# The first MLP layer of the last block as seven half products, with the bank's halves shared by two engines

## The chip, the cores and the metric

The kernel runs on 1 core of one Trainium2 chip (trn2). The metric is the device time of one execution in microseconds (us). Engines are called PE (TensorE matmul), PEld (its weight loads), DVE (VectorE), ACT (ScalarE), POOL (GpSimd) and SP (the engine whose queue issues most transfers).

## The reference

Pooled attention, then a residual MLP block over tokens (batch 8, 576 tokens, 512 features):

```python
a1 = alpha1 * x + beta1                       # x: the attention's output, (8, 576, 512)
tok = np.einsum('ts,bsd->btd', w_tok, a1)
u = x + lam * tok
a2 = alpha2 * u + beta2
ch = np.maximum(a2 @ w_ch1, 0.0) @ w_ch2      # w_ch1: (512, 2048), w_ch2: (2048, 512)
return (u + lam * ch).astype(np.float32)
```

The change concerns `np.maximum(a2 @ w_ch1, 0.0)` for the last 512 tokens. Beta2's share is a column of biases, `bias_cols`, and alpha2 is multiplied into the weights.

## The kernel before

The 8 x 576 tokens are cut into 36 chunks of 128 and the chunks into `NBLK` = 9 blocks of 512 tokens. For each block n the kernel runs the first MLP layer and then the second. While block n runs its MLP, the attention of batch n + 1 is worked in between; blocks 7 and 8 (the last) have no attention beside them any more.

The order is written out by hand: the loop over n (L943 to L1019) collects pairs (due time, function) in `todo`, sorts them, and calls the functions in that order. Every engine runs its own instructions in that order, and the framework puts in semaphore waits where two instructions touch the same tile. A due time is only a place in the order.

**First layer, `mlp_A` (L652).** The inputs are `u_fm[n]` (features on partitions, four tiles cc of 128 features, 512 tokens, bf16) and the weights `w1` in three tensors. Hidden unit group j (16 groups of 128) takes four matmuls (L662) of 512 columns into one PSUM bank `ps_h` from a ring of six (`gp`), then one ScalarE ReLU (L669) of 128x512 into `H4[n, j // 4]` (bf16). PSUM has six banks in the ring `gp` and two in a ring "ch".

**Second layer (from block `FIRST` = 2 on).** It is done in seven half products: `weight_sum` (L723, done once) and `hidden_sum` (L744) build sums of quarter matrices on VectorE, `product` (L758) runs 16 matmuls (L785) of 256 columns for each of seven products, so 112 for a block, and `gather` (L789) adds a PSUM bank to the residual `u_sb` (L803 of 512 columns, L800 of 256). `hidden_sum` S3, S1, S2, S4 exist for g = 0 (hidden groups 0 to 3 and 8 to 11) and g = 1 (4 to 7 and 12 to 15); each is one VectorE instruction (L754) of 128x1024 bf16, some in place in the hidden tiles.

In the last block the order of the products is 1, 2, 6, 5, 7, 4, 3; the output is stored in parts, and the last transfer ends the execution.

In the first layer of block 8 nothing but matmuls, ReLUs and hidden sums of g = 0 runs; at its start VectorE does the last two gathers of block 7.

Of the kernel before, what the change touches and what calls it, by code (L numbers as in the profile page):

```python
# [7 lines left out]
FP = mybir.dt.float32  # L8
F16 = mybir.dt.float16
BF = mybir.dt.bfloat16  # L10
AF = mybir.ActivationFunctionType
ALU = mybir.AluOpType
AX = mybir.AxisListType

P = 128
SPG = 72
DM = 512
DFF = 2048
NJ = DFF // P
# [4 lines left out]
def kernel(  # L24
# [18 lines left out]
    nc = tc.nc  # L43
    ctx.enter_context(tc.manual_schedule())
    B, H, S, D = q.shape

    const = ctx.enter_context(tc.tile_pool(name="const", bufs=1))
    work = ctx.enter_context(tc.tile_pool(name="work", bufs=1))
    psA = ctx.enter_context(tc.tile_pool(name="psA", bufs=6, space=bass.MemoryType.PSUM))
    psB = ctx.enter_context(tc.tile_pool(name="psB", bufs=2, space=bass.MemoryType.PSUM))  # L50

    def gp(name):
        return psA.tile([P, 512], FP, tag="gp", name=name)
# [8 lines left out]
    NBLK = len(chunks) // 4  # L62
# [156 lines left out]
    start = const.tile([1, 2], FP, tag="start", name="start")  # L219
# [38 lines left out]
    for i in range(4):  # L258
        if i < 2:
            t = const.tile([SPG, 4, 66], F16, tag=f"vp1_{i}", name=f"vp1_{i}")  # L260
            nc.vector.memset(t, 8.0)
            vp1_pool.append(t)
            t = const.tile([P, 2, 4, SPG], BF, tag=f"kpT_{i}", name=f"kpT_{i}")
# [3 lines left out]
    for i in range(2):  # L267
        t = const.tile([SPG, 4, S + 64], F16, tag=f"ET_{i}", name=f"ET_{i}")
# [8 lines left out]
                            op0=ALU.mult)  # L277
    nc.vector.tensor_tensor(out=pool_vr[0:32, 64:72], in0=pool_v[0:32, 0:16:2],
                            in1=pool_v[0:32, 1:16:2], op=ALU.add)
# [65 lines left out]
    def setup_wtok_odd():  # L345
# [6 lines left out]
    w1 = [const.tile([P, 4, 512 * (w1_at[i + 1] - w1_at[i])], BF, tag=f"w1_{i}", name=f"w1_{i}")  # L352
          for i in range(3)]
    w2 = [const.tile([P, 4, DM], BF, tag=f"w2_{g}", name=f"w2_{g}") for g in range(4)]

    def w1_of(cc, j):
        g = j // 4
        t, c0 = (w1[0], 512 * g) if g < 2 else (w1[g - 1], 0)
        return t[:, :, c0:c0 + 512].rearrange("p c (m i) -> p c i m", i=4)[:, cc, j % 4, :]
# [17 lines left out]
    bias_cols = const.tile([P, NJ], FP, tag="bias_cols", name="bias_cols")  # L377
# [209 lines left out]
    u_fm = {}  # L587
# [56 lines left out]
    H4 = {}  # L644
# [6 lines left out]
    def mlp_A(n, j, t0=0, t1=512):  # L651

        if t0 == 0:
            ps_A[j] = gp("ps_h")
        ps_h = ps_A[j]
        one = t1 < 512
        for cc in range(4):
            if n == 0:
                rhs = u_fm[0][:, cc, 0, 0:257] if one else u_fm[0][:, cc, t0 // 256:2, 0:256]
            else:  # L660
                rhs = u_fm[n][:, cc, :]
            nc.tensor.matmul(out=ps_h[:, t0:t1 + one], lhsT=w1_of(cc, j), rhs=rhs,  # L662
                             start=(cc == 0), stop=(cc == 3))
        if one:
            nc.vector.tensor_copy(out=bias_cols[:, j:j + 1], in_=ps_h[:, 256:257])  # L665
            return
        if (n, j // 4) not in H4:
            H4[n, j // 4] = work.tile([P, 4, 512], BF, tag="H4", bufs=4, name="H4")
        nc.scalar.activation(out=H4[n, j // 4][:, j % 4, :], in_=ps_h, func=AF.Relu,  # L669
                             bias=bias_cols[:, j:j + 1], scale=1.0)  # L670

    ps_ch = {}

    def mlp_B(n, m, part):
# [69 lines left out]
    def hidden_sum(n, i, g):  # L744

        lo, hi, S2, S3 = H4[n, g], H4[n, g + 2], wino["S2"][g], wino["S3"][g]
        top, low = slice(0, HALF), slice(HALF, DM)
        o, a, b, op = {
            3: (S3, lo[:, :, top], lo[:, :, low], ALU.subtract),
            1: (lo[:, :, low], lo[:, :, low], hi[:, :, low], ALU.add),  # L750
            2: (S2, lo[:, :, low], lo[:, :, top], ALU.subtract),
            4: (lo[:, :, top], hi[:, :, top], S2, ALU.subtract),
        }[i]
        nc.vector.tensor_tensor(out=o, in0=a, in1=b, op=op)  # L754
# [34 lines left out]
    def gather(n, i, part=0):  # L789

        U = u_of[n]
        top, low = slice(0, 2), slice(2, 4)
        L, R = slice(0, HALF), slice(HALF, DM)
        rows, cols = {1: ((top, L),), 2: ((top, L),), 4: ((low, L),), 5: ((low, R),),
                      6: ((top, R),), 3: ((top, R),), 7: ((low, R), (low, L))}[i][part]
        key = {1: "V", 6: "V", 7: "V", 2: "X", 4: "Y", 5: "Z", 3: "Z"}[i]
        if key == "Z" and n == NBLK - 1:
            for pp in range(2):
                o = U[:, rows.start + pp, cols]
                nc.vector.tensor_tensor(out=o, in0=o, in1=banks[key][pp], op=ALU.add)  # L800
            return
        o = U[:, rows, cols]
        nc.vector.tensor_tensor(out=o, in0=o, in1=banks[key, "both"], op=ALU.add)  # L803
# [138 lines left out]

    for n in range(NBLK):  # L943
        todo = []
        for j in range(0 if n else 4, NJ):
            if n == 0 and j < 8:
                todo.append((j, lambda j=j: mlp_A(0, j, 0, 256)))
                todo.append((j + (1.01 if j < 7 else 0.3), lambda j=j: mlp_A(0, j, 256, 512)))
            else:
                at = 8 * (j // 4 % 2) + 4 * (j // 8) + j % 4 if n >= FIRST else j  # L950
                todo.append((at, lambda j=j: mlp_A(n, j)))
# [19 lines left out]
        if n >= FIRST:  # L971
            last = n == NBLK - 1
            when = ((3, (4.6, 14.6)), (1, (8.6, 18.86)), (2, (8.8, 18.98)), (4, (22.3, 23.0)))
            if last:
                when = ((3, (4.6, 12.6)), (1, (8.6, 16.1)), (2, (8.8, 16.2)), (4, (18.6, 19.6)))
            for i, at in when:
                for g in range(2):
                    todo.append((at[g], lambda i=i, g=g: hidden_sum(n, i, g)))
            order = (1, 2, 6, 5, 7, 4, 3) if last else (1, 2, 4, 5, 6, 3, 7)
            for s, i in enumerate(order):  # L980
                for pp in range(2):
                    todo.append((16 + 2 * s + pp, lambda i=i, pp=pp: product(n, i, pp)))
                for part in range(2 if i == 7 else 1):
                    todo.append((17.05 + 2 * s + (1.9 if i == 1 and not last else 0) + 0.01 * part,
                                 lambda i=i, part=part: gather(n, i, part)))
            if last:
                for m in range(2):
                    todo.append((19.1, lambda m=m: store(n, m, 0, HALF)))
                    todo.append((25.2, lambda m=m: store(n, 2 + m, HALF, DM)))
                    todo.append((27.2, lambda m=m: store(  # L990
                        n, 2 + m, 0, HALF, (nc.sync, nc.scalar))))
                    todo.append((29.2, lambda m=m: store(
                        n, m, HALF, DM, ((nc.sync, nc.scalar)[m],) * 2)))
            else:
                for m in range(4):
                    todo.append((27.2 if m < 2 else 29.2, lambda m=m: store(n, m)))
# [5 lines left out]
        b = n + 1  # L1002
# [47 lines left out]
```

## Time and profile before

| | |
|---|---|
| median of 3 runs | 334.12 us (333.59 to 334.47) |
| profiled execution | 334.57 us, span of its instructions 332.9 us, mean granted clock 0.993 |
| PE busy | 325.5 us, 98% of the span, 2531 matmuls |
| DVE busy | 234.5 us, 70% |
| ACT busy | 175.6 us, 53% |
| first layer of block 7 / of block 8 | 13.81 us / 13.81 us |
| second layer of block 7 / of block 8 | 12.23 us / 12.24 us |
| from the last matmul's end to the end of the span | 3.7 us |

Times inside the profile are counted from the first instruction. The ends of matmuls are modelled: consecutive matmuls of 512 columns start 0.216 us apart though each is shown with 0.38 us, and those of 256 columns 0.11 us apart though each is shown with 0.27 us. "Slot" means the distance of the starts. PEclk is the granted share of the TensorE clock.

### The profile page before, as it was taken

The page shows a single profiled execution, that of the slowest core. Times are in us where ns is not written, and L with a number is a line of the kernel's source. Part 1 is how long each engine was busy: PE and PEld are TensorE (multiplying, and loading weights), DVE is VectorE, ACT ScalarE, POOL GpSimd, SP SyncE. Part 2 cuts the span into 40 slices and gives each one's busy share as a digit, 9 for nine tenths or more (in the row PEclk, how much of TensorE's full clock was granted, in tenths as well). Part 3 has the DMA queues.
Part 4 walks back from the last instruction along what each step waited for, and adds up shares of the span by engine and source line. Part 5 has one row for each costly group of instructions (what it writes and reads, how often), then busy time and mean ns, then how long its engine had stood idle before and what let it go on. Part 6 is the DMA issues. An engine that isn't in the chain of part 4 may idle for free.

```text
span 332.9 us, 6509 instructions
## 1 busy us (share of the span) xinstructions
PE 325.5 (98%) x2531; PEld 209.2 (63%) x2531; DVE 234.5 (70%) x485; ACT 175.6 (53%) x322; POOL 94.8 (28%) x110
## 2 busy tenths in 40 slices
PE   6999999999999999999999999999999999999995
PEld 2667754455544567656775676558765866586584
DVE  6674189999769969677967797877778783263263
ACT  3584989448522871288128812682268325703710
POOL 8667828601237001900271027102510200000000
PEclk9799999999999999999999999999999999999999
DMA  8999979994994983399549943996340045003003
GB/s 117 198 210 270 271 159 206 208 227 87 146 246 105 211 159 121 72 223 181 152 89 219 182 136 73 187 189 194 61 140 2 0 61 145 2 0 127 1 32 97
DMA packets 66472, 45.81 MB, mean 138 GB/s; under 512 B 34397, under 2 KB 57061, under 8 KB 66442
## 3 DMA queue, kind: packets, MB, share of 16 engines
q1 hardware_dynamic: 52092, 32.67, 42.8%
q0 software_dynamic: 13824, 12.40, 22.8%
q8 instruction: 20, 0.33, 0.4%
q10 hardware_dynamic: 526, 0.34, 0.4%
q14 instruction: 10, 0.08, 0.1%
HBM read 38.30 MB, written 9.44 MB: 143 GB/s over the span
## 4 chain that ended last, share of the span: by engine, by line
PE 90%; DMA 5%; DVE 2%; POOL 1%; issue 0%; SPq 0%; ACTq 0%; ACT 0%; DVEq 0%; POOLq 0%
PE ps_h L662 36%; PE ps_w L785 26%; PE ps_tok L614 11%; PE ps_ch L682 7%; DMA rem_raw<-in_k_dram 3%; PE ps_s L513 2%; PE ps_av L556 2%; DMA rem_raw<-in_q_dram 2%; PE ps_kp L445 1%; PE ps_sc L493 1%; PE ps_r L520 1%; DVE x_tm L564 1%; PE ps_av L560 1%; DVE xs L578 0%; SPq L148 0%
## 5 line engine op out<-in xcount | busy, mean ns | idle before, releaser
L662 PE MATMUL ps_h<-u_fm,w 128*128 128x512 bf16 (+2 forms) x608 | 133.7, 369 | 0.2 <-DVE bias_cols L665 0.2
L669 ACT ACTIVATE H<-ps_h,bias_cols 128x512 bf16<-128x512 f32 x144 | 98.2, 688 | 56.4 <-PE ps_h L662 55.4
L662 PEld LDWEIGHTS <-w 128*128 128x128 bf16 x608 | 65.5, 114 | 49.8 <-issue 2.4
L785 PEld LDWEIGHTS <-H 128*128 128x128 bf16 x560 | 53.5, 98 | 10.8 <-DVE u_sb L803 1.2
L622 ACT CAST u_bf<-u_sb 128x512 bf16<-128x512 f32 x32 | 19.8, 618 | 70.9 <-issue 39.9
L785 PE MATMUL ps_w<-w_l,H 128*128 128x256 bf16 x448 | 53.6, 273 | 0.0
L803 DVE TENSOR_TENSOR u_sb<-u_sb,ps_w 128x512 f32<-128x512 f32 x54 | 36.3, 682 | 17.1 <-PE ps_w L785 17.1
L578 POOL TENSOR_TENSOR xs<-x_tm,lamal_bc 128x512 bf16<-128x512 f32 x12 | 15.5, 1297 | 108.8 <-DVE x_tm L564 108.7
L614 PE MATMUL ps_tok<-xs,wtT 128*128 128x512 bf16 (+3 forms) x200 | 44.9, 380 | 0.5 <-DVE xs L578 0.5
L618 DVE TENSOR_TENSOR u_sb<-x_tm,ps_tok 128x512 f32<-128x512 f32 (+1 forms) x40 | 27.3, 682 | 10.0 <-PE ps_tok L614 9.9
L564 DVE TENSOR_TENSOR x_tm<-ps_av,rec 128x320 f32<-128x320 f32 x64 | 31.4, 491 | 2.7
L542 ACT ACTIVATE ET<-ps_s 72x512 f16<-72x512 f32 x56 | 32.3, 591 | 0.0
L614 PEld LDWEIGHTS <-wtT 128*128 128x128 bf16 (+3 forms) x200 | 17.3, 100 | 16.8 <-issue 1.1
L562 DVE RECIPROCAL rec<-ps_av 128x5 f32<-128x5 f32 x64 | 12.1, 190 | 17.0 <-PE ps_av L560 16.7
L483 DVE TENSOR_TENSOR v_u<-v_u 72x1024 f32<-72x1024 f32 (+1 forms) x24 | 22.7, 948 | 0.2
L785 PE MATMUL ps_w<-w_t,h_s 128*128 128x256 bf16 x168 | 22.6, 272 | 0.0
L682 PEld LDWEIGHTS <-H 128*128 128x128 bf16 x128 | 11.9, 98 | 13.7 <-issue 0.4
L754 DVE TENSOR_TENSOR H<-H,H 128x1024 bf16<-128x1024 bf16 x14 | 9.7, 690 | 14.3 <-ACT H L669 14.2
L785 PEld LDWEIGHTS <-h_s 128*128 128x128 bf16 x168 | 16.4, 98 | 4.1
L187 POOL TENSOR_TENSOR k_bf<-k_raw 128x512 bf16<-128x512 f32 x14 | 18.4, 1317 | 1.1
L754 DVE TENSOR_TENSOR h_s<-H 128x1024 bf16<-128x1024 bf16 x21 | 14.4, 686 | 6.0 <-ACT H L669 5.8
L185 POOL TENSOR_TENSOR k_raw<-k_raw 128x512 f32<-128x512 f32 x14 | 18.4, 1316 | 0.6 <-DMA k_raw<-in_k_dram 0.6
(148 smaller groups left out, 369.0 us busy)
## 6 DMA issues: line engine op xcount, KB each, us to landing
out_dram<-u_sb SPq DMA_DIRECT2D x29, 256.0 KB
k_raw<-in_k_dram SPq DMA_DIRECT2D x12, 512.0 KB
v_u<-in_v_dram SPq DMA_DIRECT2D x12, 512.0 KB
q_bf<-in_q_dram POOLq DMA_DIRECT2D x16, 256.0 KB, 7.0
w<-in_moe_w_ch_dram POOLq DMA_DIRECT2D x6, 512.0 KB, 12.0
out_dram<-u_sb SPq DMA_DIRECT2D x11, 128.0 KB
w<-in_moe_w_ch_dram POOLq DMA_DIRECT2D x1, 1024.0 KB, 14.3
k_raw<-in_k_dram POOLq DMA_DIRECT2D x2, 512.0 KB, 16.7
```

The source lines that it names most:

```text
L483: nc.vector.tensor_tensor(out=out, in0=t[:, :, 0:width], in1=t[:, :, width:2 * width], op=ALU.add)
L542: nc.scalar.activation(out=o, in_=i, func=AF.Exp, bias=0.0, scale=0.125)
L564: nc.vector.tensor_tensor(out=x[:, 1 - odd:6 - odd, dd:dd + D], in0=av[:, :, 0:64], in1=rec.unsqueeze(2).to_broadcast((P, 5, D)), op=ALU.mult)
L614: nc.tensor.matmul(out=ps_tok[p0:p1], lhsT=wtT[0:kk, at, P * c:P * c + p1 - p0], rhs=xs_pool[i][0:kk, sc, :], start=(sc == 0), stop=(sc == 4))
L618: nc.vector.tensor_tensor(out=s["u"][p0:p1, :], in0=x[p0:p1, 1 + c if c < 4 else 5 - 5 * i, :], in1=ps_tok[p0:p1, 0:DM], op=ALU.add)
L622: nc.scalar.copy(out=s["u_bf"], in_=s["u"])
L662: nc.tensor.matmul(out=ps_h[:, t0:t1 + one], lhsT=w1_of(cc, j), rhs=rhs, start=(cc == 0), stop=(cc == 3))
L669: nc.scalar.activation(out=H4[n, j // 4][:, j % 4, :], in_=ps_h, func=AF.Relu, bias=bias_cols[:, j:j + 1], scale=1.0)
L682: nc.tensor.matmul(out=ps, lhsT=H_of(n, j)[:, 128 * m:128 * m + 128], rhs=(w2l if n else w2)[j // 4][:, j % 4, :], start=(j == 0), stop=(j ...
L754: nc.vector.tensor_tensor(out=o, in0=a, in1=b, op=op)
L785: nc.tensor.matmul(out=ps, lhsT=stat(j), rhs=moving(j), stop=(j == 7), start=(first and (pp == 0 or alone) and j == 0), skip_group_check=True)
L803: nc.vector.tensor_tensor(out=o, in0=o, in1=banks[key, "both"], op=ALU.add)
```

## The change

The first layer of the last block is done in seven half products too. The weight matrix is cut into quarters a11, a12 (hidden units 0 to 1023, feature halves) and a21, a22 (hidden units 1024 to 2047), the tokens' matrix into b11, b12, b21, b22 (feature halves by token halves of 256). For a pair of hidden groups r and r + 8 (r = 0 to 7) there are two PSUM banks of the ring of six: C for group r and V for group r + 8, each with a low half (tokens 0 to 255) and a high half; and a bank Y of the two others.

- `first_sum` makes four sums of weights (S1 = a21 + a22, S2 = S1 - a11, S3 = a11 - a21, S4 = a12 - S2), each in two VectorE instructions of 128x1024 bf16; `token_sum` makes four sums of tokens (T1 = b12 - b11, T2 = b22 - T1, T3 = b22 - b12, T4 = b21 - T2) of 128x512 bf16. These twelve instructions are put into block 7's order.
- `first_product(i, r)` is one of seven products, two matmuls of 256 columns each: 1 = a11 b11 into V low, 6 = S2 T2 and 7 = S3 T3 added to V low, 4 = a22 T4 added to V low after add2 has read it, 5 = S1 T1 into Y, 2 = a12 b21 added to C low, 3 = S4 b22 added to C high.
- `first_add(i, r)`, after product 1: copy V low to C low (VectorE, `i` = 0, "copy" below). After 6: C high = V low + Y ("add1"). After 7: V high = V low + Y ("add2"). Y is copied to SBUF by ScalarE (`i` = 3) first.
- `first_relu` makes the hidden tile from a whole bank, on ScalarE, or for the upper groups of r = 1 and 4 on VectorE.

In the order, round r has product 1(r), copy(r), product 7(r-1), add2(r-1), product 5(r), Y's copy (r), product 3(r-1), lower ReLU (r-1), product 6(r), add1(r), product 2(r), product 4(r-1), upper ReLU (r-1). Round 0 lacks the parts of r-1, and a ninth round has only them. The hidden sums of g = 0 of the last block get later due times (S3, S1, S2 in the rounds 5, 6 and 7), those of g = 1 follow the rounds. The changed program has 48 matmuls more, 38 VectorE instructions more and 6 ScalarE instructions more; the instructions of POOL and SP stay the same, in the same order.

```diff
@@ -668,6 +668,85 @@
             H4[n, j // 4] = work.tile([P, 4, 512], BF, tag="H4", bufs=4, name="H4")
         nc.scalar.activation(out=H4[n, j // 4][:, j % 4, :], in_=ps_h, func=AF.Relu,
                              bias=bias_cols[:, j:j + 1], scale=1.0)
+
+    fin = {}
+
+    def first_sum(i, g):
+
+        if "W" not in fin:
+            fin["W"] = [work.tile([P, 4, 2, 512], BF, tag="v_u", bufs=2, name="w1_s")
+                         for _ in range(2)]
+            fin["X"] = work.tile([P, 4, 2, 256], BF, tag="k_raw", bufs=2, name="u_s")
+        S = [fin["W"][q][:, 2 * r + g] for q in range(2) for r in range(2)]
+        cols = slice(512 * g, 512 * g + 512)
+        a11, a12 = w1[0][:, 0:2, cols], w1[0][:, 2:4, cols]
+        a21, a22 = w1[1 + g][:, 0:2, :], w1[1 + g][:, 2:4, :]
+        o, a, b, op = {1: (S[0], a21, a22, ALU.add), 2: (S[1], S[0], a11, ALU.subtract),
+                       3: (S[2], a11, a21, ALU.subtract), 4: (S[3], a12, S[1], ALU.subtract)}[i]
+        nc.vector.tensor_tensor(out=o, in0=a, in1=b, op=op)
+
+    def token_sum(i):
+
+        X, T = u_fm[NBLK - 1], [fin["X"][:, q] for q in range(4)]
+        b11, b12, b21, b22 = (X[:, 2 * r:2 * r + 2, 256 * q:256 * q + 256]
+                              for r in range(2) for q in range(2))
+        o, a, b = {1: (T[0], b12, b11), 2: (T[1], b22, T[0]), 3: (T[2], b22, b12),
+                   4: (T[3], b21, T[1])}[i]
+        nc.vector.tensor_tensor(out=o, in0=a, in1=b, op=ALU.subtract)
+
+    def first_banks():
+        fin["V"] = [gp("ps_v") for _ in range(3)]
+        fin["C"] = [gp("ps_c") for _ in range(3)]
+        fin["Y"] = [psB.tile([P, DM], FP, tag="ch", bufs=2, name="ps_y") for _ in range(2)]
+
+    def first_product(i, r):
+
+        V, C, Y = fin["V"][r % 3], fin["C"][r % 3], fin["Y"][r % 2]
+        lo, hi = slice(0, 256), slice(256, 512)
+        X, T = u_fm[NBLK - 1], fin["X"]
+
+        def weight(q, cc):
+            t = fin["W"][q // 2][:, 2 * (q % 2) + r // 4]
+            return t.rearrange("p c (m i) -> p c i m", i=4)[:, cc, r % 4, :]
+
+        for cc in range(2):
+            o, w, x = {
+                1: (V[:, lo], lambda: w1_of(cc, r), X[:, cc, lo]),
+                2: (C[:, lo], lambda: w1_of(2 + cc, r), X[:, 2 + cc, lo]),
+                3: (C[:, hi], lambda: weight(3, cc), X[:, 2 + cc, hi]),
+                4: (V[:, lo], lambda: w1_of(2 + cc, 8 + r), T[:, 3, cc]),
+                5: (Y[:, lo], lambda: weight(0, cc), T[:, 0, cc]),
+                6: (V[:, lo], lambda: weight(1, cc), T[:, 1, cc]),
+                7: (V[:, lo], lambda: weight(2, cc), T[:, 2, cc]),
+            }[i]
+            nc.tensor.matmul(out=o, lhsT=w(), rhs=x, start=(i in (1, 5) and cc == 0),
+                             stop=(cc == 1), skip_group_check=True)
+
+    def first_add(i, r):
+
+        V, C = fin["V"][r % 3], fin["C"][r % 3]
+        lo, hi = slice(0, 256), slice(256, 512)
+        if i == 0:
+            nc.vector.tensor_copy(out=C[:, lo], in_=V[:, lo])
+        elif i == 3:
+            fin["ys", r] = work.tile([P, 256], FP, tag="y_s", bufs=2, name="y_s")
+            nc.scalar.copy(out=fin["ys", r], in_=fin["Y"][r % 2][:, lo])
+        else:
+            nc.vector.tensor_tensor(out=(C if i == 1 else V)[:, hi], in0=V[:, lo],
+                                    in1=fin["ys", r], op=ALU.add)
+
+    def first_relu(r, upper):
+
+        n, j = NBLK - 1, r + 8 * upper
+        if (n, j // 4) not in H4:
+            H4[n, j // 4] = work.tile([P, 4, 512], BF, tag="H4", bufs=4, name="H4")
+        src, dst = fin["V" if upper else "C"][r % 3], H4[n, j // 4][:, j % 4, :]
+        if upper and r in (1, 4):
+            nc.vector.tensor_scalar(out=dst, in0=src, scalar1=bias_cols[:, j:j + 1], scalar2=0.0,
+                                    op0=ALU.add, op1=ALU.max)
+        else:
+            nc.scalar.activation(out=dst, in_=src, func=AF.Relu, bias=bias_cols[:, j:j + 1],
+                                 scale=1.0)
 
     ps_ch = {}
 
@@ -942,7 +1021,25 @@
 
     for n in range(NBLK):
         todo = []
-        for j in range(0 if n else 4, NJ):
+        if n == NBLK - 2:
+            for s, i in enumerate((1, 3, 2, 4)):
+                for g in range(2):
+                    todo.append((1.3 + 2.2 * s + 1.1 * g, lambda i=i, g=g: first_sum(i, g)))
+                todo.append((10.3 + 1.1 * s, lambda i=i: token_sum(i)))
+        if n == NBLK - 1:
+            todo.append((-1, first_banks))
+            for r in range(9):
+                steps = [(0, "p", 1, r), (0.1, "a", 0, r), (0.2, "p", 7, r - 1),
+                         (0.3, "a", 2, r - 1), (0.4, "p", 5, r), (0.5, "a", 3, r), (0.6, "p", 3, r - 1),
+                         (0.7, "h", 0, r - 1), (0.8, "p", 6, r), (0.9, "a", 1, r),
+                         (1.0, "p", 2, r), (1.2, "p", 4, r - 1), (1.3, "h", 1, r - 1)]
+                for dt, kind, i, t in steps:
+                    if 0 <= t < 8:
+                        todo.append((1.8 * r + dt, {
+                            "p": lambda i=i, t=t: first_product(i, t),
+                            "a": lambda i=i, t=t: first_add(i, t),
+                            "h": lambda i=i, t=t: first_relu(t, i)}[kind]))
+        for j in range(0 if n else 4, 0 if n == NBLK - 1 else NJ):
             if n == 0 and j < 8:
                 todo.append((j, lambda j=j: mlp_A(0, j, 0, 256)))
                 todo.append((j + (1.01 if j < 7 else 0.3), lambda j=j: mlp_A(0, j, 256, 512)))
@@ -972,7 +1069,7 @@
             last = n == NBLK - 1
             when = ((3, (4.6, 14.6)), (1, (8.6, 18.86)), (2, (8.8, 18.98)), (4, (22.3, 23.0)))
             if last:
-                when = ((3, (4.6, 12.6)), (1, (8.6, 16.1)), (2, (8.8, 16.2)), (4, (18.6, 19.6)))
+                when = ((3, (9.3, 16.05)), (1, (11.1, 16.1)), (2, (12.9, 16.2)), (4, (18.6, 19.6)))
             for i, at in when:
                 for g in range(2):
                     todo.append((at[g], lambda i=i, g=g: hidden_sum(n, i, g)))
```

## The prediction

> **What bounds the kernel now.** I read the page first, then the chain of waits in order of time for the end of the span, then the busy times by stage, then single rows for prices. The page says that TensorE is the bound, at full clock to the end:
>
> ```profile
> PE 325.5 (98%) x2531; PEld 209.2 (63%) x2531; DVE 234.5 (70%) x485; ACT 175.6 (53%) x322; POOL 94.8 (28%) x110
> PEclk9799999999999999999999999999999999999999
> ```
>
> The chain shows the last two blocks (start, length, what):
>
> ```profile
> 277.09 13.81 PE ps_h L662 x64
> 290.90 12.23 PE ps_w L785 x112
> 303.13 13.81 PE ps_h L662 x64
> 316.94 12.24 PE ps_w L785 x112
> 329.19 0.02 issue
> 329.21 0.42 DVE u_sb L800
> ```
>
> Each block is a first layer (L662, 64 matmuls of 512 columns, 13.81/64 = 0.216 us each) and a second layer (L785, 112 of 256 columns, 12.24/112 = 0.109 us each). There is no hole: every microsecond cut from or put into the last first layer moves the end. VectorE in these two stages is far from full:
>
> ```profile
> 277.09:290.90 13.81, 13.81 (x67) 7.25 (x65) 4.05 (x6) 10.31 (x15) 0.00 (x0) 1.00 0.29 83
> 303.13:316.94 13.81, 13.81 (x67) 7.30 (x65) 4.05 (x6) 10.30 (x15) 0.00 (x0) 1.00 0.23 73
> ```
>
> (Columns: the stretch and its length, then busy time of PE, PEld, DVE, ACT and POOL with the number of instructions, PE clock, DMA share, GB/s.) What the change makes of the last layer is a loop in which TensorE and VectorE hand one bank to and fro. One such round trip is already in the trace, in block 0:
>
> ```profile
> 30.38 0.50 PE L662 MATMUL ps_h<-u_fm,w 128*128 128x257 bf16 x3
> 30.91 0.16 DVE L665 COPY bias_cols<-ps_h 128x1 f32<-128x1 f32 x1 [0.51 <-PE ps_h L662]
> 31.10 0.38 PE L662 MATMUL ps_h<-u_fm,w 128*128 128x256 bf16 x2 [0.23 <-DVE bias_cols L665]
> ```
>
> The last of three matmuls (0.11 apart, 0.27 long) starts at 30.60; its slot is over at 30.71; DVE starts at 30.91, 0.20 later; DVE ends at 31.07 and the next matmul starts 0.03 after that. So a VectorE step of length d between two matmuls that need it in turn costs TensorE 0.20 + d + 0.03. Here d is that of 256 fp32 columns from PSUM, 0.42 (L800 in the chain above), which makes 0.66 us.
>
> **The change, part by part.**
>
> *Matmuls removed and added.* Out go 64 at 0.216 = 13.81; in come 7 x 2 x 8 = 112 of 256 columns at 0.110 (slots of L662 with 256 columns and the same strided weights, block 0) = 12.3. Weight loads of this layout (114 ns) keep 0.033 apart in block 0's bias matmuls of one column, so they don't set the pace. Gain: 1.5 us.
>
> *Sums moved into the block ahead.* Eight weight sums of 128x1024 bf16 at 0.69 (L754 rows, same shape) and four token sums of half that (at most 0.69): 5.5 to 8.3 us on VectorE under block 7, which has 26.0 - 10.6 = 15.4 us free there (4.05 + 6.53 busy). Four stand ahead of the first hidden sum: VectorE is free of block 6's gathers at 278.4 and done with them at 280.8, before that sum's inputs come (281.3). The token sums read u_fm of block 8, whose last transpose was issued at 277.0, and stand at about 287. They add no DMA; SP's and POOL's order is unchanged. Cost 0. Without that cover: if each weight sum took the 1.75 us of the slowest such row (L742, while GpSimd worked; it is idle here), all twelve plus three hidden sums end near 298, and product 5 of block 7 (296) waits some 2.5 us.
>
> *Rounds of the last first layer.* Per r TensorE issues, in order: product 1(r), 7(r-1), 5(r), 3(r-1), 6(r), 2(r), 4(r-1), each 0.22, together 1.54. VectorE issues copy(r) (V low to C low), add2(r-1) (into V high), add1(r) (into C high). In the built program the first matmul of product 6(r) waits for copy(r), and the first of product 2(r) waits for add1(r), because both write bank C. From the start of a round: copy starts at 0.22 + 0.20 = 0.42, ends 0.84; product 6 is due at 0.88, no stall; product 6's slot ends at 1.10, add1 starts at 1.30, ends 1.72; product 2 starts at 1.76. Nothing stands between products 6 and 2 on TensorE, and product 4(r-1) and the whole next round are queued behind. **Stall 0.66 in each of 8 rounds: 5.3 us.**
>
> A rule bears on this. The row first: the round trip above, 0.66. The Trainium skill, "Perfetto Trace Analysis", section Matmuls, says that independent groups should rotate through PSUM banks so that evacuation overlaps the next group. The three V and three C banks do so; by that rule alone this term would be near 0 and the time 336.3. But "PSUM — Partial Sum Buffer", section Terms, makes a TensorE write and a VectorE access to one bank at once an error. By that the wait on bank C can't be dropped though the halves differ, and no row of this trace shows two engines in one bank at once. I keep 0.66 from the row.
>
> *Start of the rounds.* Two gathers of block 7 stand ahead of copy(0) on VectorE (DVE L803, two in 1.28 from 303.17, so one per 0.60). Copy(0) can start at 304.37 and ends at 304.79. Products 1(0) and 5(0) fill 302.97 to 303.41, product 6(0) starts at 304.83: stall 1.42.
>
> *Longer VectorE steps in between.* Two upper ReLUs (r = 1, 4; 512 columns from PSUM, 0.69 like L803, holding the engine 0.60) wait for product 4 at the end of a round, start 0.20 into the next, hold copy from 0.42 to 0.80: 0.38 each. The three hidden sums of g = 0 (0.69, held 0.60) stand between add2 and add1: copy 0.42, add2 0.75, sum 1.08, add1 1.68 instead of 1.30: 0.38 each. Five make 1.9. These assume that ready steps follow each other 0.09 before the recorded end, as the two gathers do (1.28 for two of 0.69); without it all steps together cost 1.2 more.
>
> *End of the rounds.* Product 4(7) waits for add2(7), which waits for product 7(7): done at 0.42, add ends 0.84, product 4 at 0.88 instead of 0.44: 0.44.
>
> *ScalarE.* 8 copies of 256 columns (0.37 by the 256-column COPY and exponentials) and 14 ReLUs of 0.69 are 12.6 us in over 21: not the bound. The copy for round r starts at about 0.89 and ends at 1.27, just ahead of add1. If it took 0.6, and a ReLU 0.8, the layer would lose 0.7 more.
>
> *Second layer and end.* Hidden sums of g = 1 wait for the last ReLUs 0.2 and 0.9 us after the first layer, as now (317.70 and 318.43), and S2 is needed 3.5 us into the second layer. Unchanged: 0, at most 0.4.
>
> **Sum.** 12.3 + 1.42 + 5.28 + 1.90 + 0.44 = 21.3 in place of 13.8: +7.5. The profiled execution took 334.57 (span 332.9 and 1.7 around it), so 342.1; the median 334.12 is 0.45 lower, so 341.6. I put **341.7**. Pieces of 256 columns at 0.36 to 0.50 (a shorter PSUM copy, a PSUM write that costs more; no row writes a 256-column fp32 piece into PSUM) move it by -1.0 to +1.6: the likeliest case's own range is 340.6 to 343.3.
>
> **The rivals.**
>
> *Clock drop.* TensorE will be idle about 40% of this layer. The trace shows the clock granted at half after a thin stretch:
>
> ```profile
> 6.00:8.00 2.00, 1.09 (x12) 0.68 (x12) 1.29 (x6) 0.91 (x2) 2.00 (x4) 1.00 1.39 211
> 10.00:11.00 1.00, 0.88 (x4) 0.35 (x5) 0.54 (x2) 0.54 (x2) 0.93 (x3) 1.00 1.45 196
> 11.00:12.00 1.00, 1.00 (x7) 0.89 (x8) 0.97 (x2) 0.80 (x3) 0.75 (x2) 0.52 1.45 196
> ```
>
> It stays near 0.5 for some 3.4 us. At half rate a round is about 3.7 instead of 2.2, so 3.4 us lose 1.4. One or two such drops: 343.1 to 344.5. Against it: single stalls like those here (0.39 at 30.7, 0.49 at 55.0 us) left it at 1.00, so what counts is how many come together, and the round keeps TensorE at work for 1.5 of 2.2 us. The Trainium skill, "TensorE: Matmul & The Clock Gate", Part 1, lets the clock fall only after about 3.4 us of idleness; by that a stall of at most 1.4 drops nothing and the sum stays. The row disagrees: the drop at 11.0 came with no idle stretch of TensorE above 0.91 us before it. 17%.
>
> *Narrower waits.* If product 2 could go after copy(r) alone, add1 would have the time of products 2, 4 and 1 to end, the plain rounds would cost almost nothing, and what is left is the start (1.4 + 0.2), six late steps (0.27 to 0.49) and about 0.1: 12.3 + 4.0 = 16.3, +2.4, 336.5. Against it: the built wait. 10%.
>
> *Faster.* One mechanism: VectorE's half-width steps turn round within TensorE's other products, so that TensorE runs at its matmul pace. Then only the matmul term is left: 334.1 - 1.5 = 332.6. It decides when all stalls together are under 1.5; the start alone, behind two gathers, is 1.42, so product 2 would have to wait for nothing in all 8 rounds. 5%, and 2% for a balance within 0.3%.
>
> *Sums not hidden* in block 7: 342 + 0 to 2.5, as priced above. 4%.
>
> **How the numbers follow.** The likeliest case 62%, then 17, 10, 5 + 2 and 4%. The range 339.5 to 345.0 holds the first, the clock case and the sums, with some room below for shorter round trips; it leaves out the narrower waits and the faster side. A measurement of this kernel tells about 0.3% (1 us) from no change: faster 0.05, same 0.02, slower 0.93.
>
> **What would show it.** In the profile after: the first layer of block 8 some 21 us long with PE busy well under 0.7 of it; product 2's first matmul idle for about 0.66 with the half add (PSUM bank C) as what it waited for, eight times; one idle stretch of 1.4 at its start behind L803; the second layer still 12.2; block 7 still 26.0. If those waits are on ScalarE, or the idle per round is under 0.3, or block 7 grows, the matching step is wrong. If PEclk falls in the last slices, the clock case holds.

## The result, and the profile after

The changed kernel takes 341.85 us (median of 6 runs, 340.95 to 344.69) against 333.4 us before (median of 6, 332.63 to 334.47): 1.0262 times as long, 95% interval 1.0221 to 1.0303. It is slower by 8.4 us. The forecast was 341.7 us, and 7.6 us slower than the median that it started from.

The profiled execution of the changed kernel took 340.95 us (span 339.2). The page: VectorE has 17 us more work, and TensorE is no longer full at the end.

```profile
PE 325.2 (96%) x2579; PEld 213.5 (63%) x2579; DVE 251.3 (74%) x523; ACT 176.4 (52%) x328; POOL 94.1 (28%) x110
PE   8999999999999999999999999999999999976695
PEclk9999999999999999999999999999999999999999
```

In the row of TensorE's busy tenths the hole (7, 6, 6) lies in the slices 36 to 38, from about 297 to 322 us. The clock row beside it stays at 9, so nothing in that hole is a slower TensorE.

Line numbers after the new functions are larger: L785 is now L864 (second layer), L803 is L882 and L800 is L879 (gathers). New are L722 (first_product), L730 (copy), L735 (add1 and add2), L733 (Y's copy) and L745, L748 (ReLUs). The chain of waits (start, length, what) from block 7 on:

```profile
275.23 13.81 PE ps_h L662 x64
289.04 12.24 PE ps_w L864 x112
...
301.30 1.28 DVE u_sb L882 x2
302.59 0.35 DVE ps_c L730
302.94 0.04 issue
302.99 0.39 PE ps_v L722 x2
303.38 0.04 DVEq L735
303.42 0.04 issue
303.46 0.45 DVE ps_c L735
303.90 0.04 issue
303.95 0.38 PE ps_c L722 x2
...
323.34 12.24 PE ps_w L864 x112
```

Block 7 has kept its 13.81 and 12.24 us, and so has the second layer of block 8. Between 301.28 and 323.34 the chain no longer runs along TensorE: it goes from TensorE (product 6, `ps_v`) to VectorE (add1, `ps_c L735`) and back to TensorE (product 2, `ps_c L722`), once in every round. The busy times by stage (the columns are those of the prediction):

```profile
275.23:289.04 13.81, 13.81 (x66) 7.25 (x65) 10.27 (x18) 10.31 (x15) 0.00 (x0) 1.00 0.29 83
301.28:323.34 22.06, 14.30 (x114) 12.24 (x113) 13.68 (x31) 10.90 (x21) 0.00 (x0) 1.00 0.15 46
```

In the first row VectorE has 10.27 us where it had 4.05: the sums, under an unchanged 13.81. In the second, TensorE is busy for 0.65 of the stage, VectorE for 0.62 and ScalarE for 0.49: none of the three is full. That is how a stage looks that is set by hand-overs. TensorE's waits in it (us in total, times, longest):

```profile
PE ps_c L722 <- DVE ps_c L735: 5.6, 8, 0.9
PE ps_v L722 <- DVE ps_c L730: 1.9, 3, 1.3
PE ps_v L722 <- DVE ps_v L735: 0.3, 1, 0.3
```

The first line is product 2 behind add1, eight times. The second is product 6 behind copy: the start and the two rounds in which VectorE did a ReLU. The third is product 4(7) behind add2(7). These idle times are counted from the modelled ends of matmuls, some 0.16 us after the slot is over, so the stalls below, taken between starts, are that much larger. One hand-over in the timeline:

```profile
305.07 0.38 PE L722 MATMUL ps_v<-u_s,w_s 128*128 128x256 bf16 x2
...
305.54 0.43 DVE L735 TENSOR_TENSOR ps_c<-ps_v,y_s 128x256 f32<-128x256 f32 x1 [0.20 <-PE ps_v L722]
306.03 0.27 PE L722 MATMUL ps_c<-u_fm,w 128*128 128x256 bf16 x1 [0.58 <-DVE ps_c L735]
```

Product 6's second matmul starts at 305.18 and its slot ends at 305.29. Add1 starts 0.25 later, takes 0.43, and product 2 starts 0.06 after that: 0.74 us without a TensorE slot.

Between the starts of matmuls the layer takes 22.07 us (13.81 before). Against the terms of the prediction:

| term | predicted | measured |
|---|---|---|
| 112 matmuls | 12.3 | 12.2 (0.109 each) |
| start, behind two gathers | 1.42 | 1.45 |
| product 2 behind add1, 8 rounds | 8 x 0.66 = 5.28 | 8 x 0.74 = 5.94 |
| two ReLUs on VectorE | 0.76 | 0.47 + 0.47 = 0.94 |
| three hidden sums on VectorE | 1.14 | 3 x 0.305 = 0.92 |
| tail, product 4(7) | 0.44 | 0.47 |
| five stalls of 0.03 at product 6 | none | 0.16 |
| layer | 21.3 | 22.07 |

The layer is 8.26 us longer, and the medians are 8.45 apart. The two profiled spans differ by 6.3 only, because the profile of before had a stretch of half clock from 11.0 to 14.5 us, which that of after had not: block 7 starts 1.9 us earlier in it.

### The profile page after: what moved, and what is told of

It is laid out like the page before. It is cut to its first block, busy times and chain, and to the rows that moved or that the text cites. A ratio compares the mean times of both kernels' runs of the same rounds, so it can differ in the third digit from the quotient of the medians.

```text
span 339.2 us, 6669 instructions
## 1 busy us (share of the span) xinstructions
PE 325.2 (96%) x2579; PEld 213.5 (63%) x2579; DVE 251.3 (74%) x523; ACT 176.4 (52%) x328; POOL 94.1 (28%) x110
## 4 chain that ended last, share of the span: by engine, by line
PE 82%; DMA 6%; DVE 5%; POOL 4%; issue 1%; DVEq 0%; POOLq 0%
PE ps_h L662 29%; PE ps_w L864 25%; PE ps_tok L614 11%; PE ps_ch L761 7%; DMA w<-in_moe_w_ch_dram 3%; DMA wt_bf<-in_moe_w_tok_dram 3%; PE ps_s L513 2%; PE ps_v L722 2%; PE ps_av L556 2%; PE ps_c L722 1%; DVE ps_c L735 1%; POOL k_raw L185 1%; POOL k_bf L187 1%; DVE x_tm L564 1%; PE ps_r L520 1%
## 5 line engine op out<-in xcount | busy, mean ns | idle before, releaser
L662 PE MATMUL ps_h<-u_fm,w 128*128 128x512 bf16 (+2 forms) x544 | 119.7, 367 | 0.2 <-DVE bias_cols L665 0.2
L669 ACT ACTIVATE H<-ps_h,bias_cols 128x512 bf16<-128x512 f32 x128 | 87.2, 688 | 40.6 <-PE ps_h L662 39.9
L662 PEld LDWEIGHTS <-w 128*128 128x128 bf16 x544 | 58.2, 114 | 43.5 <-issue 2.4
L864 PEld LDWEIGHTS <-H 128*128 128x128 bf16 x560 | 53.5, 98 | 10.6 <-DVE u_sb L882 1.2
L864 PE MATMUL ps_w<-w_l,H 128*128 128x256 bf16 x448 | 53.6, 273 | 0.0
L882 DVE TENSOR_TENSOR u_sb<-u_sb,ps_w 128x512 f32<-128x512 f32 x54 | 36.3, 683 | 16.9 <-PE ps_w L864 16.9
L562 DVE RECIPROCAL rec<-ps_av 128x5 f32<-128x5 f32 x64 | 12.2, 190 | 16.8 <-PE ps_av L560 16.5
L864 PE MATMUL ps_w<-w_t,h_s 128*128 128x256 bf16 x168 | 22.6, 272 | 0.0
L864 PEld LDWEIGHTS <-h_s 128*128 128x128 bf16 x168 | 16.4, 98 | 4.1
L556 PEld LDWEIGHTS <-ET 72*128 72x128 f16 x256 | 13.9, 97 | 6.4 <-DVE vp L477 0.6
L79 POOL DMA_DIRECT2D q_bf<-in_q_dram x16 | 12.6, 791 | 14.7 <-DVE v_u L158 13.9
```

The source lines that it names most:

```text
L864: nc.tensor.matmul(out=ps, lhsT=stat(j), rhs=moving(j), stop=(j == 7), start=(first and (pp == 0 or alone) and j == 0), skip_group_check=True)
```

## The experiments

Eleven kernels were run. "Layer" is the first layer of block 8, between the first matmul starts of its two layers; the time is the median.

**Add1 behind product 2.** Theory A: the order product 6, add1, product 2 costs a round trip per round, because product 2 waits for add1. Theory B: the time is that of VectorE's added work or of PSUM traffic.

```diff
-                         (0.7, "h", 0, r - 1), (0.8, "p", 6, r), (0.9, "a", 1, r),
+                         (0.7, "h", 0, r - 1), (0.8, "p", 6, r), (1.05, "a", 1, r),
```

> The half add into C high (add1) is put behind product 2 in every round, so that product 2 waits for the copy alone. Theory A (each round is a chain: product 6, add1, product 2, tied by bank C): the 0.74 us stall ahead of product 2 goes; add1 now starts behind product 2, 0.22 us later than now, and product 7 of the same r waits for it, which is 0.29 us in the plain rounds; with the late steps the layer falls from 22.1 to about 18.0 us and the time from 341.9 to about 337.8 us. Theory B (VectorE has too much to do: 24 half-width and 5 longer steps): the same steps in the same number, so no change, 341.9 us.

Measured: 337.76 us (ratio to before 1.0136, 1.0092 to 1.018), layer 18.19. No work was taken out, and 3.9 us went: theory A. The wait of product 2 is gone, and a smaller one has come at the next product that needs add1, product 7 (which overwrites the V low that add1 reads):

```profile
PE ps_v L722 <- DVE ps_c L735: 1.6, 7, 0.4
```

**The high half of C in a bank of its own.** Was it the order, or the bank that add1 and product 2 share? Here the order is the changed kernel's. Three V banks, two for C low, two for C high (`ps_d`) and one Y make the eight; the lower ReLU becomes two instructions.

```diff
-        fin["C"] = [gp("ps_c") for _ in range(3)]
-        fin["Y"] = [psB.tile([P, DM], FP, tag="ch", bufs=2, name="ps_y") for _ in range(2)]
+        fin["C"] = [gp("ps_c") for _ in range(2)]
+        fin["D"] = [gp("ps_d"), psB.tile([P, DM], FP, tag="ch", bufs=2, name="ps_d")]
+        fin["Y"] = [psB.tile([P, DM], FP, tag="ch", bufs=2, name="ps_y")]
...
-                3: (C[:, hi], lambda: weight(3, cc), X[:, 2 + cc, hi]),
+                3: (D[:, hi], lambda: weight(3, cc), X[:, 2 + cc, hi]),
...
-            nc.vector.tensor_tensor(out=(C if i == 1 else V)[:, hi], in0=V[:, lo],
+            nc.vector.tensor_tensor(out=(D if i == 1 else V)[:, hi], in0=V[:, lo],
```

> The order of the changed kernel is kept; only the high half of C (what add1 writes and product 3 adds to) gets a PSUM bank of its own, so that product 2 (C low) and add1 (C high) share no bank any more. Three V banks, two for C low, two for C high and one Y make the eight; the lower ReLU becomes two instructions of 256 columns on ScalarE. Theory A (product 2 waits for add1 only because both lie in one bank): the eight product-2 waits leave; product 7 of the next round then waits the rest of add1, since it overwrites V low which add1 reads, as in the kernel that put add1 behind product 2: first layer 17.7 to 18.3 us instead of 22.1, time 337.3 to 337.9. Theory B (the wait comes from the data or from the order itself): layer stays at 22, time 341.9. If two C pairs instead of three bring a wait of their own, it shows at product 3 or copy, and the layer lies in between.

Measured: 336.57 us (1.0096, 1.0061 to 1.0131), layer 17.20. That is 4.9 us less than the changed kernel with the same products in the same order, so the wait came from the place that product 2 and add1 share and not from the data: the two halves hold different data. That place is one tile that fills one bank; which of the two, tile or bank, brings the wait was not separated. It is better than expected, and than the kernel with another order: there add1 still had to wait for product 2, now its predecessor in the same bank; here it doesn't. TensorE's waits:

```profile
PE ps_v L723 <- DVE ps_c L731: 1.7, 3, 1.3
PE ps_v L723 <- DVE ps_d L736: 0.9, 3, 0.4
...
```

Product 2 (`ps_c` as the waiting tile) is not among them any more. Whether the wait in the shared bank could be left out was not tried either.

**One more VectorE step, ahead of add1 or behind it.** A copy of 128x256 fp32 from PSUM, that nobody reads, was put into each round, first between product 6 and add1, then right behind add1. The work is the same, only the place differs.

```diff
+        if i == 4:
+            if "spare" not in fin:
+                fin["spare"] = work.tile([P, 256], FP, tag="k_raw", bufs=2, name="spare")
+            nc.vector.tensor_copy(out=fin["spare"], in_=V[:, lo])
...
-                         (0.7, "h", 0, r - 1), (0.8, "p", 6, r), (0.9, "a", 1, r),
+                         (0.7, "h", 0, r - 1), (0.8, "p", 6, r), (0.9, "a", 1, r), (0.85, "a", 4, r),
```

(0.95 instead of 0.85 in the second.)

> The changed kernel with one idle copy of 128x256 fp32 from V low to SBUF per round, put between product 6 and add1 on VectorE. Theory A: it holds VectorE 0.34 us on the chain, so each of the 8 stalls ahead of product 2 grows from 0.74 to about 1.08 us (1.05 to 1.39 where a hidden sum stands there): the layer 22.1 + 2.7 = 24.8 us, the time about 344.5 us. Theory B (total work on VectorE sets the pace): 8 x 0.34 = 2.7 us more too, and the same amount in the next experiment.

> The same idle copy put behind add1 instead of ahead of it. Theory A: VectorE is idle 0.7 to 0.9 us there in each round, so nothing moves: the layer 22.1 us (at most 0.3 more), the time about 341.9 us. Theory B: 2.7 us more, as with the copy ahead.

Measured, one run each: ahead 347.85 us, layer 28.86; behind 343.05 us, layer 23.33. TensorE's wait for add1, ahead and then behind:

```profile
PE ps_c L722 <- DVE ps_c L739: 8.0, 8, 1.2
```

```profile
PE ps_c L722 <- DVE ps_c L739: 5.6, 8, 0.9
```

Behind add1 the copy costs nothing: 5.6 as without it. Ahead, it costs (8.0 - 5.6) / 8 = 0.30 a round, less than its 0.42, since steps that are ready follow each other ahead of the recorded end (two gathers of 0.68 take 1.28). So VectorE's work as such is not the bound; what stands in the way of add1 is. But both layers are longer than these waits explain, by 4.4 us (28.86 against 22.07 + 2.4) and 1.3 us (23.33 against 22.07). The busy times by stretch of the kernel with the copy ahead show why:

```profile
301.10:305.13 4.03, 1.82 (x17) 1.51 (x15) 2.52 (x6) 0.37 (x1) 0.00 (x0) 1.00 0.80 259
305.13:318.78 13.65, 10.69 (x49) 6.97 (x48) 6.42 (x17) 5.61 (x10) 0.00 (x0) 0.50 0.01 2
318.78:329.90 11.12, 6.40 (x51) 5.55 (x51) 7.58 (x19) 5.04 (x10) 0.00 (x0) 1.00 0.00 0
```

From 305.13 to 318.78, four times 3.41 us, the granted clock is 0.50. The kernel with the copy behind had one such stretch (305.01 to 308.42). The last section returns to it.

**The sums alone.** The kernel before with the twelve sums in block 7, and nothing that reads them.

```diff
-        if n == NBLK - 1:
+        if n == NBLK:
             todo.append((-1, first_banks))
...
-        for j in range(0 if n else 4, 0 if n == NBLK - 1 else NJ):
+        for j in range(0 if n else 4, NJ):
```

(and the due times of the hidden sums of before)

> The kernel before, with the twelve sums of weights and tokens made in block 7 and not used. Theory A (the sums lie in free VectorE time): both layers of block 7 together 26.0 us as before, the time within 1 us of 333.4. Rival (the sums push the hidden sums of block 7 late, or slow what runs beside them): block 7 longer by up to 2.5 us, 334.5 to 336.

Measured: 333.65 us beside 333.43 for the kernel before, ratio 1.0018 (0.9982 to 1.0055), block 7 at 13.81 + 12.23, block 8 at 13.81. The sums cost nothing that shows.

**One gather ahead of copy(0).** Block 7's products end with 7, 3 instead of 3, 7.

```diff
-            order = (1, 2, 6, 5, 7, 4, 3) if last else (1, 2, 4, 5, 6, 3, 7)
+            order = ((1, 2, 6, 5, 7, 4, 3) if last else (1, 2, 4, 5, 6, 7, 3) if n == NBLK - 2
+                     else (1, 2, 4, 5, 6, 3, 7))
```

> Block 7's products end with 7, 3 instead of 3, 7, so that one gather of 512 columns instead of two stands ahead of copy(0) on VectorE (the output stores change places with them). If the start stall is VectorE's queue of two gathers, it falls by the one gather, 0.6: 1.45 to 0.85, first layer 22.07 to 21.45, time 341.2. If it is something else (the banks of the ring, a first use of the summed weights), it stays at 1.45.

Measured, one run: 343.09 us, layer 21.46. The start is as expected, one gather shorter (longest wait 0.7 instead of 1.3), but the time is not:

```profile
PE ps_v L722 <- DVE ps_c L730: 1.3, 3, 0.7
PE ps_w L864 <- DVE u_sb L882: 0.8, 1, 0.8
```

The second line is new: block 7's second layer takes 13.16 instead of 12.23. Product 7 now comes right behind product 6 and writes the same bank, and the gather of that bank stands between them: the very round trip that the experiment was about, made in another place. The other 1 us by which it missed is covered by a stretch of half clock at 11.2 us, which the profile of after doesn't have; block 7 starts 1.8 us later here.

**No long VectorE steps in the rounds.** All upper ReLUs on ScalarE, and the hidden sums of g = 0 behind the rounds.

```diff
-        if upper and r in (1, 4):
+        if False:
...
-                when = ((3, (9.3, 16.05)), (1, (11.1, 16.1)), (2, (12.9, 16.2)), (4, (18.6, 19.6)))
+                when = ((3, (15.75, 16.05)), (1, (15.8, 16.1)), (2, (15.85, 16.2)), (4, (18.6, 19.6)))
```

> All upper ReLUs on ScalarE and the three hidden sums of g = 0 behind the rounds, so that VectorE does nothing in the rounds but copy, add1 and add2. If the long VectorE steps cost what the profile of the changed kernel shows (0.46 + 0.47 for the two ReLUs, 0.93 to 1.05 instead of 0.74 at product 2 for the three sums), the first layer goes from 22.07 to 20.3; the second layer then waits about 1.0 for S2 at its product 6: net -0.7, time 341.1. If the rounds' length is not set by these steps, the layer stays near 22 and the time rises by 1.

Measured, one run: 341.36 us, layer 21.51, and 1.06 us of wait in the second layer. The ReLU stalls and the longer waits behind the sums are gone (the eight waits for add1 have 0.6 as their longest, 0.9 before), and the given-back 1.06 is as expected. The layer is 1.2 longer than expected, and its trace has one half-clock stretch, 304.94 to 308.35, in which all matmuls are half as fast. So the price of the late steps is confirmed by the single waits, not by the length of the layer.

**Product 2 a round later.** The round's order becomes 1(r), 5(r), 7(r-1), 3(r-1), 2(r-1), 6(r), 4(r-1).

```diff
-                steps = [(0, "p", 1, r), (0.1, "a", 0, r), (0.2, "p", 7, r - 1),
-                         (0.3, "a", 2, r - 1), (0.4, "p", 5, r), (0.5, "a", 3, r), (0.6, "p", 3, r - 1),
-                         (0.7, "h", 0, r - 1), (0.8, "p", 6, r), (0.9, "a", 1, r),
-                         (1.0, "p", 2, r), (1.2, "p", 4, r - 1), (1.3, "h", 1, r - 1)]
+                steps = [(0, "p", 1, r), (0.1, "a", 0, r), (0.2, "p", 5, r), (0.3, "a", 3, r),
+                         (0.4, "p", 7, r - 1), (0.5, "a", 2, r - 1), (0.6, "p", 3, r - 1),
+                         (0.7, "p", 2, r - 1), (0.75, "h", 0, r - 1), (0.8, "p", 6, r),
+                         (0.9, "a", 1, r), (1.0, "p", 4, r - 1), (1.1, "h", 1, r - 1)]
```

> Order of a round: product 1(r), 5(r), 7(r-1), 3(r-1), 2(r-1), 6(r), 4(r-1), with copy, Y's copy, add2, the lower ReLU and add1 behind the products they follow; same 112 matmuls. Product 2 of a pair of groups then stands a whole round behind the add1 it shares a bank with. Theory A (the time is the PE-VectorE-PE round trips, of which add1 in front of product 2 is the one per round): 0.74 x 8 leave, only the start (1.4), the late steps behind sums and ReLUs and a short tail stay: first layer 17.0 to 17.2 us instead of 22.1, time 336.8. It also goes below the 18.2 of the kernel that only put add1 behind product 2, since there product 7 took over part of the wait. Theory B (VectorE's and ScalarE's total work or PSUM traffic in the layer sets the time): layer stays at 18 or more, time 338 or more. No half-clock stretch in the layer, because PE is at work for 0.72 of it.

Measured: 336.66 us (1.0093, 1.0057 to 1.0129), layer 17.00. Theory A again, to 0.1 us. The plain rounds take 1.61 us instead of 2.30, and in the list of TensorE's waits in the layer none is for add1 (`ps_c L735`):

```profile
PE ps_v L722 <- DVE ps_c L730: 1.5, 2, 1.3
PE ps_v L722 <- DVE ps_v L735: 1.2, 3, 0.6
```

The same 112 matmuls in another order, or in other banks, save 5 of the 8.4 us.

**All cures.** The last order, one gather ahead of the rounds, copy(0) on ScalarE, products 1(1) and 5(1) in round 0, no ReLU on VectorE, hidden sums in the rounds 6 and 7 and behind them.

```diff
-            nc.vector.tensor_copy(out=C[:, lo], in_=V[:, lo])
+            (nc.vector.tensor_copy if r else nc.scalar.copy)(out=C[:, lo], in_=V[:, lo])
...
+                    if r == 1 and (kind, i) in (("p", 1), ("p", 5), ("a", 0), ("a", 3)):
+                        dt = {"p1": -1.35, "a0": -1.3, "p5": -1.25, "a3": -1.2}[f"{kind}{i}"]
...
-                when = ((3, (9.3, 16.05)), (1, (11.1, 16.1)), (2, (12.9, 16.2)), (4, (18.6, 19.6)))
+                when = ((3, (11.95, 16.05)), (1, (13.75, 16.1)), (2, (15.8, 16.2)), (4, (18.6, 19.6)))
```

> All cures together: the order with product 2 late, one gather ahead of copy(0), copy(0) on ScalarE, products 1(1) and 5(1) pulled into round 0, all upper ReLUs on ScalarE, hidden sums of g = 0 in the rounds 6 and 7 and behind them. By the measured round trips the first layer is then 14.6 us: 12.24 of matmuls, 1.4 of start, about 1 of late steps, against 13.81 in the kernel before: time 334.3, so 0.85 slower than before, within what can be told from no change at the edge. If round trips are hidden better than that (matmul pace), 13.0 and 332.6, faster than before; if VectorE or ScalarE becomes the bound, 16 or more and 335.7.

Measured: 336.63 us (1.0072, 1.0039 to 1.0105). The layer is 14.57, as expected, though not all its parts are: the late steps come to 1.1, but the start stall is 0.75 and not 1.4, and small stalls of 0.03 and 0.06 in the plain rounds, which the expectation had not, add 0.46. The time is 2.3 above the expectation. 0.93 of it is block 7's second layer, 13.17, with the round trip of the experiment with one gather, which the expectation had left out. For the rest, 7 of its 12 runs had a mean clock of 0.985 to 0.995; the five from 0.998 up have a median of 335.1. In the next kernel block 7's products go in the last block's order, so that another product stands between 6 and 7:

```diff
-            order = ((1, 2, 6, 5, 7, 4, 3) if last else (1, 2, 4, 5, 6, 7, 3) if n == NBLK - 2
-                     else (1, 2, 4, 5, 6, 3, 7))
+            order = (1, 2, 6, 5, 7, 4, 3) if n >= NBLK - 2 else (1, 2, 4, 5, 6, 3, 7)
```

(and the due times of block 7's hidden sums, and of the gather of its product 1, to go with it)

> The kernel with all cures, but block 7's products in the last block's order 1, 2, 6, 5, 7, 4, 3 instead of 1, 2, 4, 5, 6, 7, 3. There product 7 stood right behind product 6 on the same bank and waited for the gather between them, and block 7's second layer took 13.16. If that round trip is the whole of the 0.93, the second layer of block 7 is 12.23 again, the last first layer stays at 14.57, and the time is 0.93 lower than that of the kernel with all cures. If the 0.93 belongs to the single gather at the end, it stays at 13.16.

Measured: 334.09 us (1.0008, 0.9987 to 1.003). That is 2.5 below the median of the kernel with all cures, and 1.0 below the 335.1 of its five runs near full clock; 0.93 was expected. The chain shows the second layer of block 7 at its old length again, so the 0.93 was the round trip and not the single gather:

```profile
289.45 12.24 PE ps_w L864 x112
```

The layer is 14.57 again.

**Seven products for the pairs 1 to 6 only.** The pairs 0 and 7 are done with 8 matmuls of 512 columns each, placed where VectorE is late. The rest is as in the last kernel, but for four things: copy(1) is on ScalarE, products 1(1) and 5(1) keep their place, the upper ReLU of pair 7 is on VectorE, and the hidden sums have other due times.

```diff
+    def first_plain(r, upper):
+
+        for cc in range(4):
+            nc.tensor.matmul(out=fin["V" if upper else "C"][r % 3], lhsT=w1_of(cc, r + 8 * upper),
+                             rhs=u_fm[NBLK - 1][:, cc, :], start=(cc == 0), stop=(cc == 3))
...
+            for at, upper, r in ((2.22, 0, 0), (2.75, 1, 0), (12.85, 0, 7), (13.75, 1, 7)):
+                todo.append((at, lambda upper=upper, r=r: first_plain(r, upper)))
+                todo.append((at + 0.01, lambda upper=upper, r=r: first_relu(r, upper)))
...
-                    if 0 <= t < 8:
+                    if 0 <= t < 8 and t not in (0, 7):
```

> As the last, but the pairs of hidden groups 0 and 7 are done with plain products (8 matmuls of 512 columns, 1.73 us a pair) and only the pairs 1 to 6 with seven products (1.53 of matmuls a pair, 1.61 as the rounds came out in the kernel with all cures). The plain matmuls stand where VectorE is late: pair 0 at the start, while the gather and copy(1) end, pair 7 beside the hidden sums. Worked out from the measured slots and round trips: 2 x 1.73 + 6 x 1.61 = 13.1 and 0.3 at the end of the rounds: first layer 13.3 to 13.5 against 13.81 in the kernel before, 0.14 of it given back in the second layer. Time 333.0 to 333.2, so 0.2 to 0.4 below the kernel before, less than can be told from no change by the times; the layers of the profile can tell it. If the round trips are not covered, 14 or more.

Measured: 333.67 us beside 333.65, ratio 0.9996 (0.9974 to 1.0017): no difference that can be told. In the profile the layer is 13.24 (13.81 before; 13.3 to 13.5 expected), and 0.22 is given back in the second layer (12.46; 0.14 expected), so the two layers are 0.35 us shorter than before. The chain now runs along TensorE from the start of the layer, with plain matmuls (L728) where the start stall was:

```profile
303.76 0.22 PE ps_v L722 x2
...
304.19 0.86 PE ps_c L728 x4
305.06 0.22 PE ps_v L722 x2
305.28 0.86 PE ps_v L728 x4
```

No version was faster than the kernel before by more than a measurement can tell.

## Why the prediction was right

- *What bounds the layer.* Right. The hand-over TensorE, VectorE, TensorE on bank C set the length: the same products in separate banks took 4.9 us less, in another order 5.1 less, and equal VectorE work cost 0.30 a round ahead of add1 and nothing behind it.
- *The round trip's price.* Mis-sized: 0.66 predicted, 0.74 measured in the five rounds without a hidden sum, and 1.05 (0.74 and the sum's 0.305) in the other three. Over eight rounds that is 0.66 us of the 0.77 us by which the layer was missed. The 0.42 of the step and the way of thinking held (0.43). The ends were 0.25 + 0.06 instead of 0.20 + 0.03. The round trip in block 0, from which they were taken, was a copy that waits for TensorE alone. The chain shows a step of 0.04 on VectorE's sequencer (DVEq) ahead of add1, which copy has not; add1 needs two engines, TensorE for product 6 and ScalarE for Y's copy. It is not that ScalarE was late: in rounds 0 and 3 Y's copy had ended 1.1 and 0.3 us before product 6's slot was over, and add1 still started 0.25 behind it. Add2(7), the same kind of instruction with TensorE alone left to wait for, has no such step and started 0.20 behind product 7's slot. That leaves the second wait as what costs the 0.04; no run took it away.
- *Late steps.* Right in number, and in place but for one (the hidden sum of round 6 ran ahead of add2 and not behind it, at the same cost); sizes off in both directions: a ReLU on VectorE is a tensor_scalar of 0.75 and not the 0.69 of a gather (0.47 instead of 0.38), a hidden sum costs 0.305 instead of 0.38.
- *Start and tail.* Right: 1.45 and 0.47 (1.42 and 0.44). With one gather less the start fell by its 0.60.
- *Sums under block 7, second layer.* Right: both at 0, in the changed kernel and alone.
- *ScalarE.* Right: no wait for it in the list.
- *The sum.* The layer's 8.26 us against 7.5 predicted. The predicted time came nearer (341.7 against 341.85) because the kernel before ran at 333.4 here and not at 334.12: part of that closeness is luck.
- *The rivals.* Narrower waits: not in the changed kernel, but the kernel with C in two banks is that case, and its 336.57 stands beside the 336.5 worked out for it. That closeness is luck in part, since its layer was 17.20 and not 16.3: the plain rounds kept stalls of 0.09 to 0.10, add1's and ReLU's late steps 0.3 to 0.6. Faster: it needed all stalls together below 1.5 us, and they were 9.9. Clock drop: not in the profile of after, but two of the six runs of the changed kernel have a mean clock of 0.995, which is about one stretch of 3.41 us at half clock each (half of 3.41 is 0.5% of 341); where it lay in them is not on record. In three of the experiments' profiles it lay in this layer (last section).

The Trainium skill, "Perfetto Trace Analysis", section Matmuls, advises rotating banks so that evacuation overlaps the next group. By it alone the prediction had 336.3 as the time, and the case's number was 341.85; with the halves of C in separate banks the same order took 336.57. In this case the rule gives the measured time only when each half that another engine works on counts as a group of its own.

## What to carry to other kernels

Count, for every PSUM bank, the hand-overs between engines that stand back to back in the order. Each cost the step plus about 0.3 us of TensorE here (0.74 for 256 columns), however idle the engines were on average, and the two halves of a tile that fills one bank counted as one. Before work is cut, look whether a bank of its own or another product in between takes the wait away: that was worth 5 of 8.4 us with the same work. A saving of 11% in matmuls (13.81 to 12.24) is 1.6 us here, and one uncovered start (1.45) is enough to lose it.

## What the runs showed of the hardware that had not been expected

The clock fell to half in thin stretches though TensorE never rested for long. In the kernel with the copy ahead it was at 0.50 for four times 3.41 us, in the one with the copy behind and the one without long steps once. In every trace here all changes of the granted clock lie whole multiples of 3.413 us apart, as on a grid. The grid lies otherwise against the program from trace to trace: the drop came 3.95, 3.08 and 3.92 us behind the layer's first matmul in these three. The 3.41 us ahead of the drop, in the first two (the third had 1.55 us of TensorE busy as well):

```profile
301.72:305.13 3.41, 1.21 (x11) 0.99 (x10) 2.18 (x6) 0.37 (x1) 0.00 (x0) 1.00 0.79 247
```

```profile
301.60:305.01 3.41, 1.55 (x14) 1.20 (x12) 2.35 (x5) 0.37 (x1) 0.00 (x0) 1.00 0.64 234
```

And the stretch in the changed kernel that takes in the start stall's end, in which and behind which the clock was 1.00. Its borders are those of that trace's own grid, counted from the clock's first record at 5.20 us:

```profile
302.15:305.57 3.42, 1.88 (x14) 1.54 (x14) 2.01 (x6) 0.55 (x2) 0.00 (x0) 1.00 0.64 192
```

The start stall of 1.45 us, TensorE's longest rest there, lies in each of them, wholly or in part (0.84 us of it in the last). With 1.21 to 1.55 us of TensorE's work in a stretch of the grid the clock fell, with 1.88 it stayed. The other traces fit for their last 50 us: of the stretches at full clock there all with 1.55 us or less were followed by half clock, and all with 1.61 or more were not (1.61: 332.10 to 335.51 in the kernel with product 2 a round later). Where the grid lies matters: from 301.60 to 305.01, across two stretches of its grid, the changed kernel has 1.55 us too, and its clock stayed at 1.00. That this is why one kernel drops in some executions and not in others is argued, not shown. One stretch cost about 1.1 to 1.3 us (4.4 / 4, and 23.33 - 22.07). The Trainium skill, "TensorE: Matmul & The Clock Gate", Part 1, names about 3.4 us of idleness as what lets the clock fall; the length agrees with the 3.41 us of each stretch, the idleness does not. Work in the stretch is not the whole rule either: at the start of the kernel before, the clock fell at 11.04 after a stretch in which TensorE was shown busy for 3.17.

```profile
7.63:11.04 3.41, 3.17 (x29) 1.59 (x30) 1.90 (x10) 1.98 (x6) 3.34 (x6) 1.00 1.46 186
```

What decides there stays open.
